# Gated linear attention and two MLPs on one core: alpha of later units in a PSUM bank, the carried state as 112-row blocks, and new shares between the engines

## The chip, the cores and the metric

The kernel runs on 1 core of one Trainium2 chip. The metric is the device time of one execution in microseconds (us), as a median of runs. The kernel before took 1007.21 us, the median of 3 runs between 1004.37 and 1009.0 us.

## What is computed

Inputs are q, k, v and alpha of shape (4 batches, 8 heads, 768 tokens, 48), and four weight matrices. First comes gated linear attention, head by head and token by token, then two MLPs with different activations:

```python
def _attn_ref(q, k, v, alpha) -> np.ndarray:
    B, H, S, D = q.shape
    state = np.zeros((B, H, D, D), dtype=np.float32)
    y = np.zeros_like(q)
    for t in range(S):
        state = alpha[:, :, t, :, None] * state + np.einsum('bhd,bhe->bhde', k[:, :, t], v[:, :, t])
        y[:, :, t] = np.einsum('bhd,bhde->bhe', q[:, :, t], state)
    return y.astype(np.float32)
...
x = np.ascontiguousarray(attn_out.transpose(0, 2, 1, 3)).reshape(B * S, H * D)
h = x @ w_in
g = np.where(h >= 1, h, np.where(h <= -1, 0.0, (h + 1) ** 2 / 4.0))
x = g @ w_out
h = x @ w_in2
out = (h * np.cos(h)) @ w_out2
```

The MLPs have 3072 tokens, a width of 384 and an inner width of 2048. Weights arrive as float64 and are rebuilt on the chip from their two 32-bit halves.

## The kernel before

The 3072 tokens are eight **units** u of 384 tokens, two per batch. Each unit has four **pairs** of heads, so there are 32 pairs, numbered m = 0 to 31; a pair holds its two heads on partitions 0 to 47 and 64 to 111 (the 112 rows of the shapes below), with the tokens along the free axis, as three chunks c of 128 tokens.

A pair runs through these steps (function `attention`). Alpha, k and q are loaded and transposed, so that channels lie on partitions. In the first two units (`TURN`) TensorE (PE) turns them into PSUM banks "h" (L520); in units 2 to 7, pairs 8 to 31, VectorE (DVE) turns them with `turn` (L508) from SBUF to SBUF, alpha to the tile "ta". `forward` (L550) is three scans, running products of alpha per chunk, to the tile F; `ends` takes the last column of each chunk and its reciprocal (fe); `last` (POOL, L576) and `backward` (L582), three reversed scans, make G. Then k is multiplied by G and q by F (`times`, L599, on POOL or DVE), and ScalarE (ACT) squares F and G for an overflow flag (L615). k goes to token order through TensorE (units 0 and 1) or through a DVE transpose and a round trip by DMA (L650, L655, L662). `scores` (L678) multiplies k by q into the banks "sc" (head 0) and "kv" (head 1); a triangular mask turns these into am, on DVE (L688), or by an ACT copy and a POOL product (L691, L694) for the (m, head) in `MASK_POOL`. `outer` (L710) makes k times v per chunk in "kv". The **state** T of a pair is carried from chunk to chunk: ACT scales the kv block of a chunk by its fe (L771 for the first chunk, L779 to the tile kf after that), DVE adds the old state times fe (L782). `within_and_before` makes the output y: per chunk two matmuls of v and am, one per head (L731), and, where there is a state, two of T and q (L736). T is 48 rows by 48 columns at the partitions of its head:

```python
for z in hrows:
    nc.tensor.matmul(
        yb.tile[z, s], lhsT=t.tile[z], rhs=d["tq"][z, s], start=False, stop=True
    )
```

The result y is split into a high part (ACT, L818) and a low part (DVE, L832), both in the reduced format of the matmuls that follow, and 16 rows of another pair are moved in by DMA (L840).

Layer 1 has 16 steps per unit (`step1`), layer 2 the same (`step2`). A step is 9 matmuls for h and 9 for the output (all L871, 128x384), since each product is made of three with high and low parts. Between them a step of layer 1 has an ACT activation (L949) and two DVE instructions (L953, L957), or, for the steps in `ACT_STEPS`, three on ACT and one on DVE (L975); then the split of the result on ACT (L902) and POOL (L907). Layer 1's weights are rebuilt on ACT, DVE and POOL (L345 to L374) while units 0 to 2 run.

The order is made before the kernel is built: class `Order` holds every operation with an engine, an assumed duration, the operations it waits for and the buffers it takes from rings, and places them one by one on the engines. The bank "sc" is a ring of 1, F, G and ta are rings of 1. `SPREAD` adds length behind each pair, which sets how far ahead of the steps that need it a pair is started. The numbers at the top (`SPREAD`, `STEP`, `K_DVE`, `Q_DVE`, `ACT_STEPS`, `MASK_POOL`) and the assumed durations so move instructions, and on the chip each engine takes them strictly in the order that came out. All DMAs are issued by one queue (SP).

Of the kernel before, what the change touches and what calls it, by code (L numbers as in the profile page):

```python
# [30 lines left out]
SPREAD = {None: 29.5, 0: 11.0, 1: 11.0, 2: 14.0, 3: 21.0}  # L31
SLACK = 0.0
STEP = 0.0
# [121 lines left out]
def gla_two_mlps(  # L155
# [51 lines left out]
    NV, NRAW = 4, 4  # L207
# [4 lines left out]
    rings.update({f"T{j}": 4 for j in range(NP)})  # L212
# [38 lines left out]
    v_b = [one.tile([P, CH, 112], F32, name=f"v{i}") for i in range(NV)]  # L251
    raw_b = [one.tile([P, R * D], F32, name=f"raw{i}") for i in range(NRAW)]
# [6 lines left out]
    def prologue():  # L259
# [22 lines left out]
    def weight(layer, kind, f, after=()):  # L282
# [94 lines left out]
        if new:  # L377
            cost = HW2 if kind == "out" else HW3 if layer == 2 else 4 * HW3
            pair_of["op"] = add("sp", cost, fetch, after, new=[rb], lat=LOAD + 1)
# [24 lines left out]
    def early_buffers():  # L404
# [17 lines left out]
        for c in range(CH):  # L422
# [4 lines left out]
            v0_ops.append(add("sp", HW3, load, use=[v0b], lat=LOAD + 1))  # L427

    def attention(m):
# [15 lines left out]
        for x, src in enumerate((alpha, k, q)):  # L445
# [24 lines left out]
            if turned:  # L470
                loads.append([add("sp", HW3, load_tokens, use=[rb], lat=LOAD)])
# [8 lines left out]
        else:  # L480
# [9 lines left out]
            v_ops = [add("sp", 2 * HW3, load_v, new=[vb], lat=LOAD)] * CH  # L490
# [14 lines left out]
        def turn(x, pool_, tag, tb):  # L505
            def fn():
                d[tag] = room(pool_, tag)
                nc.vector.transpose(  # L508
                    out=d[tag].rearrange("p (i r) -> p r i", r=R),
                    in_=d["raw", x].rearrange("p (r d) -> p r d", d=D)[:, :, 0:32],  # L510
                )
# [27 lines left out]
        else:  # L539
            a_src = ab  # L540
            ta, tk = turn(0, p1, "ta", ab), turn(1, p2, "tk", kb)

        def alphas(s):
            return (a_src.tile if turned else d["ta"])[0:K, s]
# [14 lines left out]
        fw = add("dve", CH * (0.35 if turned else 0.48), forward, [ta], new=[fb], use=[a_src])  # L559
# [31 lines left out]
        bw = add("dve", CH * (0.4 if turned else 0.57), backward, [la], use=[a_src, feb, gb])  # L591
# [19 lines left out]
        def square(i, nm):  # L611
            def fn():
                if turned and i == 0:
# [7 lines left out]
        for i, nm, xb in ((0, "F", fb), (1, "G", gb)):  # L621
            fresh = turned and i == 0
# [23 lines left out]
        else:  # L646
# [18 lines left out]
            a = add("sp", QUADS * HW3, write, [a], new=[sb], use=[gb], lat=LOAD + 0.5)  # L665
            ks = add("sp", HW3, read, [a], new=[ksb], use=[sb], lat=LOAD)
# [54 lines left out]

        def within_and_before(cs):

            def fn():
                if cs[0] == 0:
                    yb.tile = ps(tag_y)
                for c in cs:
# [16 lines left out]
                    0.12 + 0.37 * sum(1 if state[c][0] is None else 2 for c in cs),  # L744
# [7 lines left out]
        for c in range(CH):  # L752
# [8 lines left out]
            tb = buf(f"T{j}")  # L761
            r = slice(c * D, (c + 1) * D)
            t = T.get(j)

            def fresh(tb=tb):
                tb.tile = p1.tile([P, D], F32, tag=f"T{j}", name=f"T{j}", bufs=4)
                return tb.tile[0:K]

            if start:
                def first_state(c=c, r=r, fresh=fresh):  # L770
                    nc.scalar.mul(fresh(), kvb.tile[0:K, r], d["fe"][0:K, 0, c:c + 1])  # L771

                T_OP[j] = add("act", 0.185, first_state, [kv], new=[tb], use=[feb, kvb])
            else:
                sb_ = buf("kf")

                def scaled(c=c, r=r, sb_=sb_):
                    sb_.tile = p2.tile([P, D], F32, tag="kf", name="kf")
                    nc.scalar.mul(sb_.tile[0:K], kvb.tile[0:K, r], d["fe"][0:K, 0, c:c + 1])  # L779

# [558 lines left out]
```

## Time and profile before

| what | value |
|---|---|
| time, median of 3 runs | 1007.21 us (1004.37 to 1009.0) |
| the profiled execution: its own time | 1003.58 us |
| the profiled execution: its span | 1001.8 us |
| mean granted TensorE clock | 0.990 of full speed |
| PE, PEld (weight loads) busy | 96%, 89% of the span |
| DVE, ACT, POOL busy | 61%, 55%, 43% |

The profile is of one execution, 3.6 us below the median. Busy shares are means over stages that differ: in the first 57 us only attention runs, then attention and layer 1 run side by side up to about 505 us, then layer 2 and the rest of layer 1. So what an engine means for the time is read from the windows of the rows below, and what a PE instruction costs from the starts in a timeline, since matmuls overlap and a row's mean duration is longer than the distance from one start to the next.

### The profile page before, as it was taken

To read this page: it belongs to the slowest core of one execution; us is meant where nothing else is said; L and a number is where in the kernel's file an instruction comes from. 1 tells how busy PE (TensorE), PEld (TensorE's weight loads), DVE (VectorE), ACT (ScalarE), POOL (GpSimd) and SP (SyncE) were. 2 spreads that over 40 slices of the span, in tenths; PEclk is the share of its full clock that TensorE was granted. 3 is DMA by queue.
4 is the path that set the end of the run, shared out by engine and by line. 5 is a ranking of instruction groups with operands and counts; after the bars stand their busy time and mean duration, and the time that the engine had idled before them with its cause. 6 is when DMAs were issued, how large, how long until landed. Compare 5 with 4: busy or idle time off the path is not lost.

```text
span 1001.8 us, 17336 instructions
## 1 busy us (share of the span) xinstructions
PE 963.5 (96%) x6186; PEld 894.7 (89%) x6186; DVE 613.6 (61%) x1242; ACT 549.1 (55%) x1236; POOL 427.8 (43%) x458
## 2 busy tenths in 40 slices
PE   7897799899999999999999999999999999999997
PEld 5686787789889899889999999899999999999996
DVE  5989999986898568783345777533333333333332
ACT  3557455553344334433335678666666666666664
POOL 3245655654334334342226666534343434242332
PEclk9999799999999999999999999999999999999999
DMA  9765747453555136340031423000000000000000
GB/s 196 154 150 146 159 91 157 110 115 77 131 117 128 36 69 135 81 87 3 9 115 46 128 95 126 25 1 25 1 25 1 25 1 25 1 25 2 24 1 27
DMA packets 113551, 71.81 MB, mean 72 GB/s; under 512 B 71728, under 2 KB 96304, under 8 KB 113456
## 3 DMA queue, kind: packets, MB, share of 16 engines
q1 hardware_dynamic: 113456, 70.62, 29.8%
q8 instruction: 50, 0.82, 0.4%
q14 instruction: 45, 0.37, 0.1%
HBM read 58.79 MB, written 9.44 MB: 68 GB/s over the span
## 4 chain that ended last, share of the span: by engine, by line
PE 74%; DVE 5%; SPq 2%; DMA 2%; ACT 2%; issue 1%; POOL 0%; DVEq 0%; ACTq 0%; POOLq 0%
PE acc L871 30%; PE h L871 25%; PE sc L871 5%; PE kv L871 5%; PE y L871 4%; PE y L731 2%; PE y L736 2%; PE sc L678 1%; SPq L466 1%; DMA w_spare<-in_moe_w_out_dram 1%; PE kv L710 1%; DVE G L582 1%; SPq L655 1%; DVE F L550 0%; DMA raw<-in_q_dram 0%
## 5 line engine op out<-in xcount | busy, mean ns | idle before, releaser
L907 POOL TENSOR_TENSOR gl<-ang,gh 128x384 fp32r<-128x384 f32 x127 | 129.3, 1018 | 234.7 <-ACT gh L902 202.8
L907 POOL TENSOR_TENSOR gl<-r,gh 128x384 fp32r<-128x384 f32 x128 | 132.7, 1037 | 178.4 <-ACT gh L902 146.9
L871 PE MATMUL h<-x,winhi 128*128 128x384 f32 x768 | 199.5, 340 | 4.8 <-DVE r L957 2.8
L871 PEld LDWEIGHTS h<-x,winhi 128*128 128x128 f32 x768 | 138.1, 188 | 10.0 <-DVE r L957 4.2
L871 PE MATMUL acc<-gh,wouthi 128*128 128x384 f32 x384 | 135.3, 352 | 1.7 <-ACT gh L902 0.8
L871 PE MATMUL acc<-gl,wouthi 128*128 128x384 f32 x384 | 130.8, 341 | 2.6 <-POOL gl L907 2.4
L949 ACT ACTIVATE r<-h,half 128x384 f32<-128x384 f32 x119 | 69.0, 580 | 113.9 <-PE h L871 107.3
L871 PE MATMUL h<-x,winlo 128*128 128x384 f32 x384 | 130.0, 339 | 1.3 <-POOL winlo L374 1.3
L871 PE MATMUL acc<-gh,woutlo 128*128 128x384 f32 x384 | 129.9, 338 | 0.0
L902 ACT CAST gh<-r 128x384 fp32r<-128x384 f32 x128 | 65.5, 512 | 97.4 <-DVE r L957 82.7
L953 DVE TENSOR_TENSOR h<-r,h 128x384 f32<-128x384 f32 x119 | 66.5, 559 | 83.7 <-ACT r L949 83.1
L1060 ACT ACTIVATE ang<-ang 128x384 f32<-128x384 f32 x128 | 67.2, 525 | 67.3 <-DVE ang L1055 67.3
L871 PE MATMUL h<-x2s,winhi 128*128 128x384 f32 x402 | 102.3, 335 | 0.6 <-DVE ang L1067 0.5
L871 PE MATMUL acc<-wouthi,gl 128*128 128x384 f32 x288 | 98.1, 341 | 0.3 <-POOL gl L907 0.2
L871 PE MATMUL acc<-wouthi,gh 128*128 128x384 f32 x288 | 97.8, 340 | 0.5 <-ACT gh L902 0.5
L871 PE MATMUL acc<-woutlo,gh 128*128 128x384 f32 x288 | 97.3, 338 | 0.0
L902 ACT CAST gh<-ang 128x384 fp32r<-128x384 f32 x128 | 65.5, 512 | 55.7 <-DVE ang L1067 55.6
L871 PEld LDWEIGHTS acc<-gh,wouthi 128*128 128x128 f32 x384 | 72.6, 189 | 8.2 <-issue 2.1
L871 PEld LDWEIGHTS acc<-gl,wouthi 128*128 128x128 f32 x384 | 72.7, 189 | 4.4 <-POOL gl L907 4.4
L1067 DVE SCALAR_TENSOR_TENSOR ang<-ang,h 128x384 f32<-128x384 f32 x67 | 37.0, 553 | 64.5 <-ACT ang L1063 64.5
L871 PEld LDWEIGHTS h<-x,winlo 128*128 128x128 f32 x384 | 72.0, 188 | 2.3 <-POOL winlo L374 2.3
L871 PEld LDWEIGHTS h<-x2s,winhi 128*128 128x128 f32 x402 | 72.8, 188 | 1.2 <-DVE ang L1067 0.8
(164 smaller groups left out, 2105.4 us busy)
## 6 DMA issues: line engine op xcount, KB each, us to landing
w_raw<-in_moe_w_out_dram SPq DMA_DIRECT2D x18, 384.0 KB, 3.6
scr<-G SPq DMA_DIRECT2D x96, 48.0 KB, 1.9
ks<-scr SPq DMA_DIRECT2D x24, 192.0 KB, 2.7
out_dram<-o SPq DMA_DIRECT2D x24, 192.0 KB, 2.0
v<-in_v_dram SPq DMA_DIRECT2D x56, 72.0 KB, 2.4
w_raw<-in_moe_w_in_dram SPq DMA_DIRECT2D x10, 384.0 KB, 4.0
raw<-in_alpha_dram SPq DMA_DIRECT2D x48, 72.0 KB, 2.1
raw<-in_k_dram SPq DMA_DIRECT2D x48, 72.0 KB, 2.1
```

The costliest lines, as they stand in the source:

```text
L466: nc.sync.dma_start(dst[p0:p0 + 32, 0:n], bass.AP(src.tensor, off, [[R * D, 32], [1, n]]))
L582: nc.vector.tensor_tensor_scan(out=d["G"][0:K, c * C:(c + 1) * C - 1][:, ::-1], data0=alphas(slice(c * C + 1, (c + 1) * C))[:, ::-1], data ...
L655: nc.sync.dma_start(scr[:, 32 * z:32 * z + 32].rearrange("(m i) d -> i m d", i=32), d["G"][32 * z:32 * z + 32].rearrange("p (m d) -> p m d ...
L731: nc.tensor.matmul(yb.tile[z, s], lhsT=vcols(c, z), rhs=am_b[amb.slot][:, e, s], start=True, stop=t is None)
L736: nc.tensor.matmul(yb.tile[z, s], lhsT=t.tile[z], rhs=d["tq"][z, s], start=False, stop=True)
L871: nc.tensor.matmul(o, lhsT=lhs[a], rhs=rhs[b], start=first and i == 0, stop=last and i == 2)
L902: nc.scalar.copy(ghb.tile, g())
L907: eng.tensor_tensor(out=glb.tile, in0=g(), in1=ghb.tile, op=ALU.subtract)
L949: nc.scalar.activation(rb.tile, h.tile[:, 0:N], AF.Relu, bias=half, scale=0.5)
L953: nc.vector.tensor_tensor(out=hh, in0=rb.tile, in1=hh, op=ALU.max)
L1060: nc.scalar.activation(rb.tile, rb.tile, AF.Sin, scale=HALF_TURN)
L1067: nc.vector.scalar_tensor_tensor(out=rb.tile, in0=rb.tile, scalar=1.0, in1=h.tile[:, 0:N], op0=ALU.subtract, op1=ALU.mult)
```

## The change

Four things change.

1. In units 2 to 7 alpha is turned by DVE into the PSUM bank "sc" instead of the SBUF tile "ta", and the six scans of a pair read it there. The bank is the one that the scores of the pair use later, a ring of 1.
2. The state of a pair is one block of 112 rows by 2 x 48 columns, with zeros where rows of one head meet columns of the other. The two state matmuls of a chunk take all 112 rows each; ACT scales head by head, two instructions of 48 rows where there was one of 112, and DVE advances 96 columns where there were 48. The blocks and kf are persistent tiles that POOL sets to zero at the start.
3. The tables are set anew. Pair 6 has k, and pairs 2 and 3 have q, on DVE, and pair 7 has q no longer; step 13 of unit 1 is no longer an ACT step; the masks of POOL go from 7 to 9; for pairs 25, 28, 30 and 31 (`LOW_POOL`) the low part of y is made by an ACT copy and a POOL subtraction; `SPREAD` goes from 29.5 to 25, for unit 2 from 14 to 20, for unit 3 from 21 to 15; assumed durations of DMA issues, scans and y steps are changed. All of these reach the chip as another order alone.
4. The overflow check takes both heads in one pass of 112 rows.

```diff
-SPREAD = {None: 29.5, 0: 11.0, 1: 11.0, 2: 14.0, 3: 21.0}
+SPREAD = {None: 25.0, 0: 11.0, 1: 11.0, 2: 20.0, 3: 15.0}
...
-STEP = 0.0
+STEP = 0.5
...
-K_DVE = (3, 4, 5)
-Q_DVE = (0, 1, 4, 6, 7)
+K_DVE = (3, 4, 5, 6)
+Q_DVE = (0, 1, 2, 3, 4, 6)
...
-ACT_STEPS = ((4, 10, 12, 15), (1, 4, 10, 13, 14))
-MASK_POOL = ((1, 0), (6, 1), (11, 0), (13, 0), (14, 0), (15, 0), (15, 1))
+LOW_POOL = (25, 28, 30, 31)
+ALPHA_BANK = "sc"
+ACT_STEPS = ((4, 10, 12, 15), (1, 4, 10, 14))
+MASK_POOL = ((3, 0), (3, 1), (6, 1), (11, 0), (12, 1), (13, 0), (14, 1), (15, 0), (15, 1))
...
+    t_b = one.tile([P, NP + NTW, 2, D], F32, name="T")
+    kf_b = one.tile([P, 2, 2, D], F32, name="kf")
...
+        nc.gpsimd.memset(t_b, 0.0)
+        nc.gpsimd.memset(kf_b, 0.0)
...
-                d[tag] = room(pool_, tag)
+                if pool_ is None:
+                    tb.tile = ps(tb.tag)
+                    dst = tb.tile[:, 0:N]
+                else:
+                    dst = d[tag] = room(pool_, tag)
                 nc.vector.transpose(
-                    out=d[tag].rearrange("p (i r) -> p r i", r=R),
+                    out=dst.rearrange("p (i r) -> p r i", r=R),
...
-            a_src = ab
-            ta, tk = turn(0, p1, "ta", ab), turn(1, p2, "tk", kb)
+            a_src = buf(ALPHA_BANK)
+            ta, tk = turn(0, None, "alpha", a_src), turn(1, p2, "tk", kb)
...
-                        for z in hrows:
+                        for e, z in enumerate(hrows):
                             nc.tensor.matmul(
-                                yb.tile[z, s], lhsT=t.tile[z], rhs=d["tq"][z, s], start=False, stop=True
+                                yb.tile[z, s], lhsT=state_of(t)[:, e, :], rhs=d["tq"][0:K, s], start=False, stop=True
                             )
...
-                    0.12 + 0.37 * sum(1 if state[c][0] is None else 2 for c in cs),
+                    0.15 + 0.235 * sum(1 if state[c][0] is None else 2 for c in cs),
...
+            def scale_blocks(dst, c=c):
+
+                for e, z in enumerate(hrows):
+                    nc.scalar.mul(dst[z, e, :], kvb.tile[z, c * D:(c + 1) * D], d["fe"][z, 0, c:c + 1])
...
-                    nc.scalar.mul(sb_.tile[0:K], kvb.tile[0:K, r], d["fe"][0:K, 0, c:c + 1])
...
-                        out=fresh(),
-                        in0=t.tile[0:K],
+                        out=state_of(tb),
+                        in0=state_of(t),
                         scalar=d["fe"][0:K, 0, c:c + 1],
-                        in1=sb_.tile[0:K],
+                        in1=kf_b[0:K, sb_.slot],
...
-        lo = add("dve", k_ * dve(N), low, [hi], use=[yb, stb if first else xb])
+        if m in LOW_POOL:
+            ycb = buf("ta")
+            a = add("act", act(N), copied, [hi], new=[ycb], use=[yb])
+            lo = add("pool", k_ * pool(N), low_pool, [a], use=[ycb, stb if first else xb])
+        else:
+            lo = add("dve", k_ * dve(N), low, [hi], use=[yb, stb if first else xb])
```

The order moves at two places that matter below. The first is DVE in the middle of attention, around the scans of one pair of units 2 to 7. A row is a line, an operation, and out<-in; am is the masked scores, ta or sc holds alpha. Before:

```order
L550 SCALAR_TENSOR_TENSOR F<-ta,big 112x128 x3
L563 TENSOR_SCALAR fe<-F 112x3
L953 TENSOR_TENSOR h<-r,h 128x384
L688 TENSOR_TENSOR am_93<-sc,mask 128x384
L688 TENSOR_TENSOR am_93<-kv,mask 128x384
L569 RECIPROCAL fe<-fe 112x3
L957 SCALAR_TENSOR_TENSOR r<-r,h 128x384
L582 SCALAR_TENSOR_TENSOR G<-ta,fe,big 112x127 x3
```

The same place with the change:

```order
L699 TENSOR_TENSOR am_93<-sc,mask 128x384
L519 STREAM_TRANSPOSE sc<-raw_102 128x12x32
L561 SCALAR_TENSOR_TENSOR F<-sc,big 112x128 x3
L574 TENSOR_SCALAR fe<-F 112x3
L970 TENSOR_TENSOR h<-r,h 128x384
L580 RECIPROCAL fe<-fe 112x3
L792 SCALAR_TENSOR_TENSOR T<-T,fe,kf 112x96
L974 SCALAR_TENSOR_TENSOR r<-r,h 128x384
L593 SCALAR_TENSOR_TENSOR G<-sc,fe,big 112x127 x3
```

Before, alpha of a pair stood turned, and its scans had begun, ahead of the masks of the pair in front of it; now the turning of alpha stands behind the mask that empties "sc", and the scans behind that.

The second place is ACT, where the kv blocks of a pair are scaled for two chunks. Before:

```order
L615 ACTIVATE ta,chk<-G 112x384
L615 ACTIVATE ta,chk<-F 112x384
L949 ACTIVATE r<-h,half 128x384
L779 ACTIVATE kf<-kv,fe 112x48 x2
L691 COPY am_94<-sc 128x384
```

With the change:

```order
L626 ACTIVATE ta,chk<-F 112x384
L626 ACTIVATE ta,chk<-G 112x384
L919 CAST gh<-r 128x384
L782 ACTIVATE kf<-kv,fe 48x48 x4
L966 ACTIVATE r<-h,half 128x384
```

Two instructions have become four, in the same place of the queue.

## Rows read from the trace of the kernel before

**Rows 1.** Windows: start:end, length, busy us of PE, PEld, DVE, ACT, POOL; clock, DMA.

```profile
0.00:57.00 57.00, 46.98 (x440) 34.98 (x441) 43.49 (x120) 28.76 (x81) 17.20 (x41) 0.94 0.79 166
...
75.00:225.00 150.00, 132.04 (x877) 112.42 (x876) 141.43 (x270) 82.89 (x201) 87.45 (x88) 0.97 0.59 130
225.00:525.00 300.00, 299.03 (x2080) 269.40 (x2079) 203.42 (x424) 117.80 (x279) 110.44 (x121) 1.00 0.37 82
525.00:1001.80 476.80, 467.41 (x2653) 463.29 (x2651) 209.80 (x397) 310.49 (x655) 203.11 (x202) 1.00 0.10 32
```

**Rows 2.** Waits of PE, 75 to 225 us: who for whom, total us, times, longest.

```profile
PE kv L710 <- DVE am L688: 3.6, 1, 3.6
PE h L871 <- DVE r L957: 2.8, 4, 1.5
...
PE kv L678 <- DVE am L688: 2.1, 1, 2.1
```

**Rows 3.** Timeline of PE, a pair with three states: start us, us, instruction.

```profile
503.34 0.43 PE L731 MATMUL y<-am,v 128*64 128x128 f32 x4
503.70 0.42 PE L736 MATMUL y<-tq,T 48*48 48x128 f32 x4
504.05 0.43 PE L731 MATMUL y<-am,v 128*64 128x128 f32 x4
...
505.48 0.45 PE L871 MATMUL acc<-gh,wouthi 128*128 128x384 f32 x1
```

**Rows 4.** Timeline of PE, a pair with two states.

```profile
422.37 0.65 PE L731 MATMUL y<-am,v 128*64 128x128 f32 x8
422.95 0.42 PE L736 MATMUL y<-tq,T 48*48 48x128 f32 x4
...
424.02 0.62 PE L871 MATMUL h<-x,winhi 128*128 128x384 f32 x2
```

**Rows 5.** Groups by line and form, 75 to 225 us: busy us, mean ns.

```profile
L582 DVE TENSOR_TENSOR_SCAN G<-ta,fe,big 112x127 f32<-112x127 f32 x27 | 20.4, 808 | 2.1 <-DMA scr<-G 2.1
L550 DVE TENSOR_TENSOR_SCAN F<-ta,big 112x128 f32<-112x128 f32 x24 | 14.6, 660 | 0.2 <-POOL tq L599 0.2
L953 DVE TENSOR_TENSOR h<-r,h 128x384 f32<-128x384 f32 x22 | 12.2, 554 | 0.8 <-ACT r L949 0.7
L736 PE MATMUL y<-tq,T 48*48 48x128 f32 x68 | 7.7, 305 | 1.6 <-ACT T L771 1.6
```

**Rows 6.** Groups by line and form, whole span: busy us, mean ns.

```profile
L582 DVE TENSOR_TENSOR_SCAN G<-h,fe,big 112x127 f32<-112x127 f32 x18 | 7.3, 462 | 0.0
L550 DVE TENSOR_TENSOR_SCAN F<-h,big 112x128 f32<-112x128 f32 x18 | 6.3, 405 | 4.2 <-PE h L520 4.2
L953 DVE TENSOR_TENSOR h<-r,h 128x384 f32<-128x384 f32 x119 | 66.5, 559 | 83.7 <-ACT r L949 83.1
L508 DVE STREAM_TRANSPOSE ta<-raw 128x384 f32<-128x384 f32 x24 | 20.7, 862 | 2.5 <-ACT ta L615 2.5
L650 DVE STREAM_TRANSPOSE G<-tk 128x384 f32<-128x384 f32 x24 | 13.5, 563 | 1.9 <-POOL tk L599 1.9
L782 DVE SCALAR_TENSOR_TENSOR T<-T,fe,kf 112x48 f32<-112x48 f32 x64 | 25.0, 391 | 6.0 <-ACT kf L779 4.7
L779 ACT ACTIVATE kf<-kv,fe 112x48 f32<-112x48 f32 x60 | 15.2, 299 | 5.0 <-PE kv L710 5.0
L599 POOL TENSOR_TENSOR tk<-tk,G 112x384 f32<-112x384 f32 x28 | 31.0, 1108 | 19.4 <-DVE G L582 14.7 <-PE h L871 2.8 <-PE acc L871 2.0
```

**Rows 7.** The scans of line 582 by form, whole span: ns min/median/max.

```profile
L582 DVE TENSOR_TENSOR_SCAN G<-ta,fe,big x72: 397/474/3119, 82.5 to 441.0; 112x127 f32<-112x127 f32 x72
L582 DVE TENSOR_TENSOR_SCAN G<-h,fe,big x18: 454/456/481, 6.3 to 55.9; 112x127 f32<-112x127 f32 x18
```

**Rows 8.** Timeline of POOL at the start.

```profile
1.27 0.21 POOL masks.py:65 MEMSET mask<- 128x128 f32 x1
...
6.45 0.19 POOL L576 COPY G<-fe 112x3 f32<-112x3 f32 x1 [3.05 <-DVE fe L569]
```

More of the change, by code (lines that the diff above doesn't have):

```diff
@@ L211, in gla_two_mlps @@
     rings.update({"wy": 2, "wz": 2, "ta": 1, "F": 1, "G": 1, "tq": 2, "stg": 1, "tk": 2, "ks": 2, "am": 2})
-    rings.update({f"T{j}": 4 for j in range(NP)})
+    rings.update({f"T{j}": 1 for j in range(NP)})
+    rings["Tw"] = NTW
     rings.update({"kf": 2, "fe": 3, "r": 3, "gh": 3, "gl": 3, "scr": 3})
@@ L426, in load @@
                 )
-            v0_ops.append(add("sp", HW3, load, use=[v0b], lat=LOAD + 1))
+            v0_ops.append(add("sp", 1.0, load, use=[v0b], lat=LOAD + 1))
     def attention(m):
@@ L470, in attention @@
             if turned:
-                loads.append([add("sp", HW3, load_tokens, use=[rb], lat=LOAD)])
+                loads.append([add("sp", 0.7, load_tokens, use=[rb], lat=LOAD)])
             else:
@@ L488, in load_v @@
                     )
-            v_ops = [add("sp", 2 * HW3, load_v, new=[vb], lat=LOAD)] * CH
+            v_ops = [add("sp", 2 * HW2, load_v, new=[vb], lat=LOAD)] * CH
         def vcols(c, z):
@@ L557, in forward @@
                 )
-        fw = add("dve", CH * (0.35 if turned else 0.48), forward, [ta], new=[fb], use=[a_src])
+        fw = add("dve", CH * 0.35, forward, [ta], new=[fb], use=[a_src])
         def ends():
@@ L589, in backward @@
                 )
-        bw = add("dve", CH * (0.4 if turned else 0.57), backward, [la], use=[a_src, feb, gb])
+        bw = add("dve", CH * 0.4, backward, [la], use=[a_src, feb, gb])
         def times(tag, src, by, direct, pool_, tb, by_buf, after):
@@ L612, in fn @@
             def fn():
-                if turned and i == 0:
+                if i == 0:
                     d["ta"] = room(p1, "ta")
@@ L621, in attention @@
         for i, nm, xb in ((0, "F", fb), (1, "G", gb)):
-            fresh = turned and i == 0
+            fresh = i == 0
             sq.append(
@@ L664, in attention @@
             a = add("dve", dve(N), block, [ksc, sq[1]], use=[gb, kb])
-            a = add("sp", QUADS * HW3, write, [a], new=[sb], use=[gb], lat=LOAD + 0.5)
-            ks = add("sp", HW3, read, [a], new=[ksb], use=[sb], lat=LOAD)
+            a = add("sp", QUADS * HW2, write, [a], new=[sb], use=[gb], lat=LOAD + 0.5)
+            ks = add("sp", 0.9, read, [a], new=[ksb], use=[sb], lat=LOAD)
         hrows = (slice(0, D), slice(64, 64 + D))
@@ L789, in advance @@
                     )
-                a = add("act", 0.185, scaled, [kv], new=[sb_], use=[kvb, feb])
-                T_OP[j] = add("dve", 0.29, advance, [a, T_OP[j]], new=[tb], use=[feb, t, sb_])
+                a = add(
+                    "act", 0.4, lambda sb_=sb_, f=scale_blocks: f(kf_b[:, sb_.slot]), [kv], new=[sb_], use=[kvb, feb]
+                )
+                T_OP[j] = add("dve", 0.34, advance, [a, T_OP[j]], new=[tb], use=[feb, t, sb_])
             T[j] = tb
@@ L820, in copied @@
         def copied():
-            d["yc"] = p1.tile([P, N], F32, tag="ta", name="yc")
-            nc.scalar.copy(d["yc"][0:112], yb.tile[0:112, 0:N])
+            ycb.tile = p1.tile([P, N], F32, tag="ta", name="yc")
+            nc.scalar.copy(ycb.tile[0:112], yb.tile[0:112, 0:N])
         def low_pool():
@@ L1100, in step2 @@
             a = add("dve" if c == 1 else "act", 0.47 if c == 1 else act(N), put, [ops[c]], new=[ob], use=[acc[c]])
-            add("sp", HW2, store, [a], use=[ob], lat=LOAD)
+            add("sp", 0.9, store, [a], use=[ob], lat=LOAD)
     def judge():
```

35 lines of the change are left out of this document (15 added, 20 removed).

## The prediction, written before the changed kernel had run

> **What bounds the kernel now.** The windows come first [rows 1]. PE is busy in nearly all of the span, so nothing that only relieves another engine can pay unless PE waits for it somewhere, and the windows say where it waits. From 225 to 525 us PE is busy 299.0 of 300 us and DVE 203.4: PE alone sets the pace, and a microsecond less on PE is a microsecond less in the time. After 525 us, where no attention is left, PE is busy to within about 9 us of 477, and the change touches nothing there but the place of the overflow check. From 75 to 225 us it is different: PE is busy 132.0 of 150 us, so 18.0 us are waits, while DVE is busy 141.4, 94%. The waits of PE in that stretch name DVE for 8.5 us (the masks for 3.6 and 2.1, a step's product for 2.8) [rows 2], the rest is spread thinly over POOL and ACT. So there DVE sets the pace and PE follows. Before 75 us the attention of units 0 and 1 and the first weights run, DVE is busy 43.5 of the first 57 us, PE 47.0, and PE waits for chains through all engines.
>
> **The state matmuls (PE).** The price of a y step is read from starts, not from durations. In a pair with three states, masks (L731) start at 503.34, states (L736) at 503.70, the next masks at 504.05: each group of four records takes 0.36 us, and the whole step 505.48 - 503.34 = 2.14 us [rows 3]. In a pair with two states the step begins with two mask groups in a row, from 422.37 to 422.95, 0.58 us for both [rows 4]. The second took 0.58 - 0.36 = 0.22 us: without a change of form a group costs 0.22 us, and 0.14 us is what going from 128-row tiles (128*64) to 48-row tiles (48*48), and back, costs each time. With the change the state matmuls take 112 rows and columns of 48, the same form as the masks, so all groups but the last should run at 0.22. A step of six groups then takes 5 x 0.22 + 0.36 = 1.46 us, 0.68 less; one of five takes 4 x 0.22 + 0.36 = 1.24 instead of 1.65 us [rows 4], 0.41 less. Of the 32 pairs half have three states. In 75 to 225 us there are 68 records of L736 [rows 5], 17 states, 7 pairs (three and four): 3 x 0.68 + 4 x 0.41 = 3.7 us. Eight pairs lie before, worth 4.4 us that I count at nothing, since PE waits there anyway; if it does not, they count in full. After 225 us there are 17 pairs (nine and eight): 9 x 0.68 + 8 x 0.41 = **9.4 us**, all on the path.
>
> **The scans (DVE).** From 75 to 225 us the scans of alpha in SBUF keep DVE busy 20.4 us (27 of G, mean 808 ns) and 14.6 us (24 of F, mean 660 ns) [rows 5]. Units 0 and 1 make the same scans from PSUM: 18 of G in 7.3 us and 18 of F in 6.3 us, 0.41 and 0.35 us each [rows 6]. The medians hardly differ, 474 against 456 ns; the difference is a few very long ones, up to 3119 ns from SBUF and none over 481 from PSUM [rows 7]. POOL was less busy when the PSUM ones ran (17.2 of 57 us, against 87.5 of 150), so that alone does not clear them. But L953, which also has one operand in PSUM, runs in the busy stretch at 554 ns, no slower than its 559 over the whole span [rows 5, 6]. So I take the PSUM price: 27 x 0.41 + 24 x 0.35 = 19.4 us, and 35.0 - 19.4 = 15.6 us less on DVE. The 48 more columns of a state cost little: 384 columns take 559 ns, 48 take 391 [rows 6], 0.5 ns a column, so two advances for each of eight pairs cost 16 x 0.024 = 0.4 us. One mask fewer and one step product more on DVE cancel. DVE then needs 141.4 - 15.6 + 0.4 = 126.2 us for this work.
>
> [...]
>
> Turning alpha into PSUM has no row. Below it is a transpose with a plain output, 563 ns, above it the present one, 862 ns [rows 6], raised once more by the ratio of these two, to 1.32 us. I keep 862, since input and output pattern stay the same. The upper end costs the nine pairs (27 scans of G) 9 x 0.46 = 4.1 us in the stretch.
>
> **What 75 to 225 us becomes.** PE needs 132.0 - 3.7 = 128.3 us, DVE 126.2. If all of PE's waits went, the stretch would take 128.3, a gain of 21.7; if none went, 146.3, a gain of 3.7. DVE now loses 150 - 141.4 = 8.6 us to its own waits; I let it lose the same again, since loads and ACT's queue stay: 126.2 + 8.6 = 134.8 us, a gain of **15.2 us**. The new order also puts the first y of unit 2 behind 228 matmuls of steps instead of 165 and with it some of DVE's work into the stretch where DVE is busy 203 of 300 us; I add nothing for that.
>
> **What I cost at nothing.** 80 more ACT instructions of about 0.3 us [rows 6] lie where ACT is busy 82.9 of 150 and 117.8 of 300 us [rows 1]; uncovered they put 0.6 us per pair between L710 and the states, with DVE's advance and PE's y behind them. The four low parts on POOL go from 0.55 us on DVE to an ACT copy and about 1.1 us on POOL, a microsecond longer for four pairs. Zeroing 960 columns on POOL, between 0.6 and 1.6 us by the 0.21 us for 128, fits in the 3.05 us that POOL waits before its first use [rows 8]. The shares of k, q and masks in units 0 and 1 move about 0.6 us to DVE net, which is not full there. No DMA is added. The overflow check loses two short DVE instructions.
>
> **The sum.** 15.2 + 9.4 = 24.6 us off the profiled execution's own 1003.58 us is 979.0. That execution was 3.6 us below the median shown, so I forecast a median of **982.6 us**.
>
> **The rivals.**
> - *DVE was not the brake.* The stretch is held by loads and by queues in fixed order, and a lighter DVE waits longer instead. For it: PE waited for DVE by name for 8.5 of the 18.0 us only [rows 2]. Then 3.7 + 9.4 = 13.1 us, 990.5, as a median 994.
> - *Everything goes.* All 18.0 us of waits vanish and the early pairs count: 21.7 + 9.4 + 4.4 = 35.5 us, 968.1, as a median 971.7. For it: after the change neither engine is full. Against it: they share fixed orders, with chains between them.
> - *The bank ties the pairs together (slower).* Alpha can now be turned only when the mask has emptied "sc", and the next scores need that bank back. The chain from scores to scores is a mask of 384 columns as L953, 0.56, turning 0.86, F 1.05, G 1.22, k on POOL 1.11, and between them two short DVE instructions, up to 0.39 as L782, and a POOL copy of 0.19 [rows 6, 8]: 5.8 us, with the scores and nine hand-offs some 7.5 as my estimate. The order leaves no more than 33 to 45 matmuls between scores in seven places; at 467.4 us for 2653 [rows 1] these are 5.8 to 7.9 us, and a little attention. Each DVE piece also queues behind step products of 0.55 us, and behind the waiting transpose stand the scans and the products of steps that PE needs. Such a place can lose 3 us, seven of them 21 us, which brings the time to about 1000. From 1.3 us a pair, over 24 pairs, the gain is gone; at 2 us it is 1003.6 - 24.6 + 48 = 1027. Against it: in PE's stretch most pairs lie 60 to 130 matmuls apart.
> - *The 112-row blocks do not run side by side (slower).* Then a state group takes 0.36 us twice, 80 groups cost 28 us more, of which 21 after 75 us, and the 13.1 us of PE do not come: 1003.6 - 11.5 + 21 = 1013, as a median 1017. Against it: the masks already run so, with 128 rows, at the pace of the 48-row states [rows 3]. [...]
>
> **How the numbers follow.** I give the forecast 0.62, DVE not the brake 0.17, everything 0.10, the tied bank 0.08 (over half of it only eating the gain), and the blocks 0.03. A difference below 0.5%, 5 us, cannot be told from no change. The first three are all faster: 0.89. The tied bank near break-even gives same 0.05; its worse half and the blocks give slower 0.06. The range reaches from 968, everything gone in a run like the profiled one, to 999, past the second case and the dear transpose.
>
> **What would show it.** In the profile after, L751 (the states) should start 0.22 us after the masks of its chunk, and a whole y step take 1.46 or 1.24 us. Scans from "sc" should have a mean near 460 and 405 ns with none over 600. PE's idle time from 75 to about 210 us should be about 6 us and not 18. I am wrong on the states if the distance is 0.36, on the scans if long ones remain, on the bank if PE waits before L689 or DVE before L519 by microseconds in many places after 225 us, and on the brake if DVE idles more while PE's waits stay.

## The result, and the profile after

The changed kernel takes **979.66 us** (median of 4 runs, 974.75 to 980.37) against 1007.85 us for the kernel before on the same chip: a ratio of 0.972, 95% interval 0.970 to 0.975. The forecast was 982.6 us, the range 968 to 999. The profiled execution took 979.92 us, its span 978.1, against a forecast of 979.0.

The windows of the changed kernel, in the columns of [rows 1]:

```profile
0.00:57.00 57.00, 41.62 (x381) 33.90 (x382) 38.55 (x108) 29.57 (x84) 15.32 (x38) 0.94 0.75 154
...
75.00:225.00 150.00, 142.01 (x970) 130.00 (x969) 130.03 (x262) 92.00 (x218) 85.08 (x88) 1.00 0.56 122
225.00:525.00 300.00, 298.64 (x2165) 280.98 (x2165) 207.69 (x456) 146.17 (x355) 127.38 (x141) 1.00 0.40 91
525.00:978.10 453.10, 446.15 (x2543) 444.63 (x2541) 201.02 (x380) 301.55 (x633) 190.63 (x190) 1.00 0.10 32
```

From 75 to 225 us PE idles 8.0 us and not 18.0, DVE is busy 130.0 and not 141.4 us, so DVE's own idle time there grew from 8.6 to 20.0 us. In the first 57 us PE is busy 5.4 us less than before.

The waits of PE in 75 to 225 us answer to [rows 2]:

```profile
PE h L888 <- DVE r L974: 3.1, 3, 1.4
PE h L888 <- DVE r L992: 1.8, 3, 0.9
PE h L888 <- ACT winhi L377: 1.2, 1, 1.2
```

The waits for masks (3.6 and 2.1 us) are gone; what is left for DVE is products of steps, 4.9 us.

The y steps, on PE's timeline: one of two states, then one of three, against [rows 4] and [rows 3]. L746 are the masks, L751 the states.

```profile
298.53 0.65 PE L746 MATMUL y<-am,v 128*64 128x128 f32 x8
299.01 0.39 PE L751 MATMUL y<-tq,T 112*48 112x128 f32 x4
...
299.77 0.37 PE L689 MATMUL sc<-tq,tk 48*128 48x128 f32 x1
...
313.00 0.43 PE L746 MATMUL y<-am,v 128*64 128x128 f32 x4
313.27 0.39 PE L751 MATMUL y<-tq,T 112*48 112x128 f32 x4
313.49 0.39 PE L746 MATMUL y<-am,v 128*48 128x128 f32 x4
...
314.47 0.37 PE L689 MATMUL sc<-tq,tk 48*128 48x128 f32 x1
```

The steps take 299.77 - 298.53 = 1.24 us and 314.47 - 313.00 = 1.47 us, where they took 1.65 and 2.14. Inside, a group of four starts 0.22 us after the last.

The scans by form over the whole span, against [rows 7] (ns min/median/max):

```profile
L593 DVE TENSOR_TENSOR_SCAN G<-sc,fe,big x72: 450/457/482, 87.6 to 470.8; 112x127 f32<-112x127 f32 x72
L561 DVE TENSOR_TENSOR_SCAN F<-sc,big x72: 358/397/426, 82.0 to 465.1; 112x128 f32<-112x128 f32 x72
```

No scan from the bank takes over 482 ns; from SBUF they went up to 3119. The DVE groups of 75 to 225 us, against [rows 5], with the rebuilding of weights beside them:

```profile
L356 DVE TENSOR_SCALAR wz<-wy 128x384 int32<-128x384 int32 x23 | 16.0, 715 | 0.2
L360 DVE SCALAR_TENSOR_TENSOR wz<-wy,wz 128x384 int32<-128x384 int32 x24 | 14.3, 619 | 0.0
L366 DVE SCALAR_TENSOR_TENSOR wz<-w_spare,wz 128x384 uint32<-128x384 uint32 x13 | 10.9, 859 | 0.0
L593 DVE TENSOR_TENSOR_SCAN G<-sc,fe,big 112x127 f32<-112x127 f32 x21 | 8.5, 460 | 0.0
...
L561 DVE TENSOR_TENSOR_SCAN F<-sc,big 112x128 f32<-112x128 f32 x21 | 7.3, 402 | 0.0
L519 DVE STREAM_TRANSPOSE tk<-raw 128x384 f32<-128x384 f32 x7 | 6.2, 882 | 0.3 <-DMA raw<-in_k_dram 0.3
...
L519 DVE STREAM_TRANSPOSE sc<-raw 128x384 f32<-128x384 f32 x7 | 4.1, 585 | 0.0
```

The same weight lines in the kernel before, same stretch:

```profile
L353 DVE SCALAR_TENSOR_TENSOR wz<-wy,wz 128x384 int32<-128x384 int32 x23 | 14.3, 653 | 0.0
...
L349 DVE TENSOR_SCALAR wz<-wy 128x384 int32<-128x384 int32 x23 | 11.4, 513 | 0.0
...
L359 DVE SCALAR_TENSOR_TENSOR wz<-w_spare,wz 128x384 uint32<-128x384 uint32 x12 | 7.3, 618 | 0.0
```

Two things stand out. Turning alpha into the bank takes 585 ns, where turning k into SBUF in the same order takes 882. And two of the weight instructions, which the change does not touch, became longer: 715 ns instead of 513, 859 instead of 618. The one between them did not: 619 ns, where it took 653.

**Where the time came from.** To compare two executions, take the start of the nth matmul of 128x384 (L871, now L888), that is, how far the MLP steps have come (us from the span's start, from the two traces):

| step matmul | 1st | 151st | 201st | 551st | 701st | 1901st | 2601st | 4601st |
|---|---|---|---|---|---|---|---|---|
| before | 57.7 | 98.1 | 118.3 | 210.0 | 242.8 | 514.7 | 641.9 | 993.3 |
| after | 66.9 | 102.8 | 111.9 | 193.8 | 228.2 | 495.4 | 618.2 | 969.7 |
| difference | +9.2 | +4.7 | -6.4 | -16.2 | -14.6 | -19.3 | -23.7 | -23.6 |

The first step comes 9.2 us later. Between the 151st and the 201st matmul 11.1 us come back at once, until the 551st another 9.8; 4.7 come by the 1901st (the end of attention) and 4.4 at the passage to layer 2, where before the rebuilding of weights and the overflow check met PE. Behind it nothing changes.

The table counts steps alone, and the two orders put different amounts of attention in front of a step. In front of the 1st step matmul PE has made the y of 7 pairs, where it had made 6; in front of the 701st of 14 and not 15, and the scores of 15 pairs and not 17. So a part of the 14.6 us at the 701st is work put off. Run 1 below, with the y steps as long as in the kernel before and the order of the changed one, takes 276.3 us from the 701st to the 1901st, where the kernel before takes 271.9: about 4.4 us were put off, and some 10 us are the stretch's own gain. The two profiled executions are 23.7 us apart, the medians 28.2, since the profiled execution of the kernel before was 3.6 us below the median that stood with it.

### The profile page after: what moved, and what is told of

Its sections match the earlier page's. It is cut to its first block, busy times and chain, and to the rows that moved or that the text cites. A ratio compares the mean times of both kernels' runs of the same rounds, so it can differ in the third digit from the quotient of the medians.

```text
span 978.1 us, 17438 instructions
## 1 busy us (share of the span) xinstructions
PE 943.6 (96%) x6186; PEld 902.2 (92%) x6186; DVE 592.0 (61%) x1237; ACT 580.9 (59%) x1318; POOL 427.1 (44%) x464
## 4 chain that ended last, share of the span: by engine, by line
PE 84%; DVE 6%; DMA 3%; ACT 2%; issue 2%; SPq 2%; POOL 0%; DVEq 0%; POOLq 0%; ACTq 0%
PE acc L888 33%; PE h L888 27%; PE sc L888 5%; PE kv L888 5%; PE y L888 5%; PE y L746 2%; PE sc L689 2%; PE h L531 2%; PE y L751 1%; PE kv L721 1%; DVE wz L356 1%; DMA raw<-in_alpha_dram 1%; DMA w_raw<-in_moe_w_in_dram 1%; SPq L473 1%; DMA ks<-scr 1%
## 5 line engine op out<-in xcount | busy, mean ns | idle before, releaser
L888 PE MATMUL h<-x,winhi 128*128 128x384 f32 x768 | 198.6, 339 | 6.2 <-DVE r L974 3.1
L888 PEld LDWEIGHTS h<-x,winhi 128*128 128x128 f32 x768 | 137.8, 188 | 10.4 <-DVE r L974 3.9
L888 PE MATMUL acc<-gh,wouthi 128*128 128x384 f32 x384 | 135.8, 354 | 0.0
L888 PE MATMUL acc<-gl,wouthi 128*128 128x384 f32 x384 | 130.0, 338 | 0.3 <-POOL gl L924 0.3
L888 PE MATMUL acc<-gh,woutlo 128*128 128x384 f32 x384 | 130.0, 339 | 0.0
L888 PE MATMUL h<-x,winlo 128*128 128x384 f32 x384 | 129.0, 336 | 0.6 <-POOL winlo L381 0.5
L888 PE MATMUL h<-x2s,winhi 128*128 128x384 f32 x402 | 103.0, 337 | 0.0
L888 PE MATMUL acc<-wouthi,gl 128*128 128x384 f32 x288 | 97.4, 338 | 0.3 <-POOL gl L924 0.3
L888 PE MATMUL acc<-wouthi,gh 128*128 128x384 f32 x288 | 96.9, 337 | 0.0
L888 PE MATMUL acc<-woutlo,gh 128*128 128x384 f32 x288 | 96.9, 336 | 0.0
L888 PEld LDWEIGHTS acc<-gh,wouthi 128*128 128x128 f32 x384 | 71.9, 187 | 6.5 <-issue 2.8
L888 PEld LDWEIGHTS h<-x2s,winhi 128*128 128x128 f32 x402 | 73.4, 188 | 0.0
L888 PEld LDWEIGHTS h<-x,winlo 128*128 128x128 f32 x384 | 72.1, 188 | 1.2 <-POOL winlo L381 1.2
L888 PEld LDWEIGHTS acc<-gl,wouthi 128*128 128x128 f32 x384 | 72.1, 188 | 0.8 <-POOL gl L924 0.8
```

The lines of the kernel that those rows point to most:

```text
L888: nc.tensor.matmul(o, lhsT=lhs[a], rhs=rhs[b], start=first and i == 0, stop=last and i == 2)
```

## The experiments

All medians are beside runs of the kernel before on the same chip; "over the changed kernel" is the difference of the two ratios to the kernel before (0.9722 for the changed one) times 1006.6 us. Each ratio is certain to 2 to 3 us, a difference of two to some 3.5.

**1. The form of the state matmuls.**

```
-  yb.tile[z, s], lhsT=state_of(t)[:, e, :], rhs=d["tq"][0:K, s], ...
+  yb.tile[z, s], lhsT=state_of(t)[z, e, :], rhs=d["tq"][z, s], ...
```

> The changed kernel, with only the state matmuls of y back to 48 rows and columns (48*48 in place of 112*48); state blocks, tables and the order of every instruction stay. Theory (each change of form between masks and states costs PE 0.14 us): the y steps take 2.14 us (three states) and 1.65 us (two) again instead of the 1.46 and 1.24 that the changed kernel shows; 17 pairs after 225 us cost 9.4 us more, the pairs before up to 8 us, part of it hidden: 9 to 17 us over the changed kernel, 989 to 997 us. Rival (the form is worth nothing in the end, because PE waits elsewhere): y steps at 2.14 and 1.65 us, time within 3 us of the changed kernel's 979.7.

992.07 us, ratio 0.9855 [0.9826, 0.9884]: 13.4 us over the changed kernel. Steps of y take 1.65 and 2.15 us again. By the starts of step matmuls, this kernel is behind the changed one by 4.6 us at the 1st, 4.3 at the 151st, 4.3 at the 551st, 5.7 at the 701st and 14.8 at the 1901st. So in this order the form is worth almost nothing from 75 to 225 us, and 9.1 us behind the 701st matmul, at 228 us. How much of the 4.6 us before the first step it is worth is not shown: the granted clock of this execution is lower there (0.81 from 57 to 75 us, where the changed kernel had 0.92, and 0.91 against 0.94 before that), and the execution is 2.7 us above the median of its kernel.

**2. Alpha in SBUF, with the planner told so.** The source of the scans becomes "ta", and the planner's ring and assumed scan durations with it; the planner then makes another order.

```
-  a_src = buf(ALPHA_BANK)
-  ta, tk = turn(0, None, "alpha", a_src), turn(1, p2, "tk", kb)
+  a_src = ab
+  ta, tk = turn(0, p1, "ta", ab), turn(1, p2, "tk", kb)
```

> The changed kernel with alpha of units 2 to 7 turned into SBUF and scanned there again; the wide states and the new tables stay. Theory (the long scans are a matter of having both operands in SBUF, and DVE paces PE in the stretch of about 75 to 225 us): scans of 600 to 3000 ns are back on the turned units, their means at 0.6 to 0.8 us, the transposes of alpha at 0.86 instead of 0.58 us, DVE needs 15 us more for the same work in that stretch, and the kernel comes 8 to 16 us above the changed kernel: 988 to 996 us. Rival (DVE was not the brake): the long scans are back, but the time stays within 3 us of 979.7.

1010.07 us, ratio 1.0029 [1.0011, 1.0047]: 31 us over the changed kernel, far more than either theory. PE's waits from 95 to 180 us:

```profile
PE acc L888 <- DVE x L1020: 8.1, 1, 8.1
PE sc L689 <- POOL tk L610: 7.2, 1, 7.2
PE h L888 <- DVE r L974: 3.4, 3, 2.5
PE kv L721 <- DVE am L699: 3.0, 2, 2.2
```

Two stalls of 7.2 and 8.1 us stand one behind the other, and the 50 step matmuls from the 151st to the 201st take 31.0 us instead of 9.1. The order changed with the place, so this run does not price the operand's place. Run 5 does.

**3 and 4. Is DVE the brake?** The transpose of q of units 2 to 7 is issued twice, in the kernel before and in the changed one.

```
+  if x == 2:
+      nc.vector.transpose(out=d[tag]..., in_=d["raw", x]...)
```

> The kernel before with the transpose of q of units 2 to 7 issued twice in a row on VectorE (the second writes the same values), nothing else moved: 0.86 us more of DVE for each of 24 pairs, about nine of them in 75 to 225 us. Theory (DVE paces that stretch): 6 to 9 us slower than the kernel before, almost all of it gathered by matmul 900 and none of it after. Rival (DVE is not the brake, the stretch is held by loads and fixed queues): less than 2 us.

> The same doubled transpose of q in the changed kernel: 0.86 us more of DVE for each of 24 pairs. Theory (with the scans short, DVE has slack and paces much less of the stretch): 0 to 4 us slower than the changed kernel, clearly less than the same edit costs the kernel before. Rival (DVE still paces the stretch as before): 6 to 9 us slower here too.

The kernel before becomes 1014.16 us, ratio 1.0080 [1.0054, 1.0105], 8.1 us slower; the changed one 980.15 us, ratio 0.9741 [0.9712, 0.9769], 1.9 us more, within the uncertainty of no change. So some 21 us more on DVE (24 transposes of 0.87) cost 8.1 us before and next to nothing now: DVE was a brake, and is almost none any more. One part of the first expectation missed: of the 10.8 us in the profiled executions 4.8 had come by the 701st matmul and another 5.9 between it and the 1901st. PE is busy 294.0 of the 300 us after 225 us there, instead of 299.0, and waits for DVE's masks for 3.7 us behind the 701st matmul: there, too, DVE held PE up in places.

**5. The place of alpha alone.** The order of every engine is that of the changed kernel, only the tile differs; the squares go to a bf16 tile so that "ta" is free.

```
-  tb.tile = ps(tb.tag)
-  dst = tb.tile[:, 0:N]
+  dst = d["ta"] = room(p1, "ta")
```

> The changed kernel with alpha of units 2 to 7 turned into the SBUF tile ta in place of the bank sc and scanned from there, every instruction of every engine in the same order as in the changed kernel (the squares of the overflow check are written to a bf16 tile of their own). So, unlike the kernel that gave the planner alpha in SBUF, only the place of the operand differs. Theory (long scans cost DVE time that PE waits for, in the stretch of about 75 to 225 us): the transposes of alpha take 0.86 us again and scans of over 600 ns are back, 7 pairs in that stretch cost DVE some 10 to 14 us, of which the idle time DVE has there hides a part: 4 to 14 us over the changed kernel, 984 to 994 us. Rival (the place is worth nothing in itself, the 30 us of the other kernel came from its order): within 3 us of 979.7.

982.61 us, ratio 0.9778 [0.9754, 0.9803]: 5.6 us over the changed kernel, near the low end of the theory. Its DVE groups of 75 to 225 us:

```profile
L593 DVE TENSOR_TENSOR_SCAN G<-ta,fe,big 112x127 f32<-112x127 f32 x21 | 13.7, 705 | 0.0
...
L357 DVE TENSOR_SCALAR wz<-wy 128x384 int32<-128x384 int32 x23 | 13.3, 597 | 0.0
L561 DVE TENSOR_TENSOR_SCAN F<-ta,big 112x128 f32<-112x128 f32 x21 | 12.0, 625 | 0.0
...
L519 DVE STREAM_TRANSPOSE ta<-raw 128x384 f32<-128x384 f32 x7 | 6.1, 865 | 0.0
```

The scans cost 25.7 us and not 15.8, the transposes 6.1 and not 4.1: 11.9 us more. The first weight instruction costs 13.3 us and not 16.0. Its window:

```profile
75.00:225.00 150.00, 140.82 (x947) 128.94 (x944) 135.02 (x258) 91.30 (x216) 87.53 (x87) 0.99 0.53 118
```

DVE is busy 135.0 us against 130.0, but the window holds a slightly different set of instructions. Since the order is the same, instructions can be compared one by one instead. Of the 409 that DVE starts before the 701st step matmul of the changed kernel, the scans and the transposes of alpha take 12.6 us more here, all the others together 3.9 us less. The 701st matmul comes only 2.4 us later (another 2.9 are lost by the 1901st): most of what DVE does more falls into time in which it was idle in the changed kernel. Over the whole kernel DVE does 25 us more, and the time grows by 5.6.

**6 to 8. Old tables in the changed kernel.** All of them (SPREAD, STEP, K_DVE, Q_DVE, LOW_POOL, ACT_STEPS, MASK_POOL), then K_DVE, Q_DVE and MASK_POOL, then K_DVE and Q_DVE alone.

```
-K_DVE = (3, 4, 5, 6)
-Q_DVE = (0, 1, 2, 3, 4, 6)
+K_DVE = (3, 4, 5)
+Q_DVE = (0, 1, 4, 6, 7)
```

> The changed kernel with the tables as before (shares of k, q and masks, SPREAD, STEP, the steps' shares, no low parts on POOL); the wide states and alpha in the bank stay. Theory (the two parts of the change pay by themselves, the tables only move the attention a little): 975 to 990 us; the first step matmul again near 58 to 60 us instead of 66.9 and the weights of the second layer meeting attention again, about 4 us lost there. Rival (the tables carry much of the gain, since alpha in the bank ties scores to scores and the old order leaves these too close): 990 to 1010 us, with PE waiting before the scores or DVE before the transpose of alpha.

> The changed kernel with the shares of k, q and masks of units 0 and 1 between DVE, POOL and ACT as before (K_DVE, Q_DVE, MASK_POOL), the rest of the change kept; steps then begin after five pairs have finished y's instead of seven. Theory (these shares and the order that follows from them delay the first steps by 9 us, and the stretch behind does not need that): the first step matmul at 57 to 62 us, 2 to 8 us faster than the changed kernel. Rival (the attention left over comes later and costs the same, or meets the DVE-bound stretch): within 3 us, or slower.

> The changed kernel with only the shares of k and q as before (K_DVE, Q_DVE), the masks' shares as in the change. Theory (the delay of the start comes from the shares of k and q): first step matmul at 57 to 62 us, 2 to 8 us faster than the changed kernel. Rival (it comes from the masks on POOL, or from the wide states): start at 65 to 68 us and the time within 3 us.

999.64 us (ratio 0.9947 [0.9929, 0.9965]), 1007.34 us (1.0016 [0.9999, 1.0034]) and 999.93 us (0.9943 [0.9923, 0.9962]): 23, 30 and 22 us over the changed kernel. In all three my theory fell. The rival held in the first two; in the third neither did, since the first step came at 69.6 us, later than in the changed kernel. (In the second the steps begin behind the y of six pairs by the trace, not five.) With all tables old, the first step comes 2.4 us earlier than in the changed kernel, not 7; by the 151st matmul this kernel is 3.4 us ahead, by the 201st 28.2 behind. The waits of the second one (old shares of k, q and masks) from 95 to 180 us, and its windows:

```profile
PE sc L689 <- POOL tq L610: 11.6, 1, 11.6
PE kv L721 <- DVE wz L366: 11.6, 1, 11.6
PE sc L689 <- POOL tk L610: 8.0, 2, 5.2
```

```profile
105.00:120.00 15.00, 1.72 (x12) 1.43 (x12) 13.58 (x30) 5.63 (x15) 6.87 (x8) 0.62 0.78 160
120.00:135.00 15.00, 4.61 (x44) 3.64 (x44) 11.89 (x29) 6.41 (x18) 6.03 (x7) 0.61 0.76 167
135.00:150.00 15.00, 7.67 (x41) 7.22 (x42) 11.17 (x26) 6.33 (x19) 8.85 (x9) 0.52 0.73 177
```

PE is busy 14.0 of these 45 us, and the granted clock is down to 0.52 to 0.62. This led to a new theory: the jam comes where the order leaves PE too few step matmuls between the scores of the first pairs of unit 2.

**9 to 11. The spacing of the scores.** One table put back at a time: MASK_POOL; STEP (to 0.0); SPREAD.

> The changed kernel with only the masks' shares as before (MASK_POOL). In its PE order 54, 75 and 120 step matmuls lie between the 9th, 10th, 11th and 12th scores (114, 84 and 111 in the changed kernel; 36 and 36 for the first and third in the kernel with the old shares of k and q, which jams). Theory (the jam of 100 to 140 us comes where fewer than about 40 step matmuls lie between the scores of the first pairs of unit 2; otherwise the order is free): no PE idle time of over 3.5 us in one place, within 5 us of the changed kernel, and up to 4 us faster since the first steps come earlier. Rival (any change of this order jams, the tables are a lottery): 10 to 30 us slower.

> The changed kernel with STEP back to 0.0 alone. In its PE order 36, 162 and 45 step matmuls lie between the 9th, 10th, 11th and 12th scores. Theory (fewer than about 40 step matmuls between the first scores of unit 2 jam): PE idle for 5 us and more in one piece between 105 and 135 us, the clock halved behind it, 10 to 25 us slower than the changed kernel. Rival (STEP is a small term of the planner's, the spacing of scores is not the cause): within 4 us.

> The changed kernel with SPREAD as before alone. In its PE order 141, 93, 96 and 36 step matmuls lie between the 9th to 13th scores. Theory (spacing of the first scores decides): no jam between 100 and 150 us; units 2 and 3 are spread otherwise, at most a short wait at the 36 behind the 12th scores; within 6 us of the changed kernel. Rival (a lottery): 10 to 30 us slower.

987.01 us (ratio 0.9799 [0.9771, 0.9826]), 998.46 us (0.9916 [0.9891, 0.9940]) and 988.58 us (0.9816 [0.9788, 0.9844]): 7.8, 19.5 and 9.5 us over the changed kernel. Only the STEP run jams early, as expected. Its two stalls of over 6 us are both of the outer products (L721), the first with 6.1 us put down to the DMA of ks, not scores waiting. The columns are the step matmuls that the order puts between the scores of pairs 8, 9, 10 and 11, and the time from the 151st to the 201st step matmul in the trace:

| kernel | 8 to 9 | 9 to 10 | 10 to 11 | 151st to 201st, us |
|---|---|---|---|---|
| changed kernel, runs 1 and 5 | 114 | 84 | 111 | 9.1, 9.2, 9.2 |
| old masks | 54 | 75 | 120 | 9.9 |
| old SPREAD | 141 | 93 | 96 | 12.3 |
| STEP 0 | 36 | 162 | 45 | 25.7 |
| old k, q | 36 | 162 | 36 | 28.1 |
| alpha in SBUF, planned so | 36 | 162 | 36 | 31.0 |
| all tables old | 36 | 225 | 33 | 40.7 |
| old k, q, masks | 27 | 0 | 0 | 53.3 |
| before | 201 | 9 | 84 | 20.2 |

With 54 or more there is no jam in this piece, with 36 or fewer always. The kernel before has its own stall there, 3.6 us for a mask of pair 8 [rows 2], and a granted clock of 0.50 behind it (105 to 114 us; 0.70 in the mean from 105 to 120 us). No run moves the spacing alone, so this is a pattern over these kernels and not a shown cause. And it does not explain all: the kernels with old masks and old SPREAD lose 7.8 and 9.5 us, more than the 5 and 6 I had allowed, and lose them further on, the first with 6.0 us in one wait for DVE at 153 us, which I had said would not come. The kernels with old SPREAD and with STEP 0 also lose the 4.4 us at the passage to layer 2 again: from the 1901st to the 2601st matmul they take 127.2 and 127.3 us, as the kernel before (127.2), and the changed kernel 122.8. So putting back either of these two tables, which move no work between engines, is enough to lose them.

**12. The wide states alone, in the order of before.** Everything else is the kernel before, the order of every engine included, but for the overflow check in one pass.

```
-  fresh(), in0=t.tile[0:K], in1=sb_.tile[0:K]
+  out=state_of(tb), in0=state_of(t), in1=kf_b[0:K, sb_.slot]
```

> The kernel before, its tables, costs and order of every engine kept, with the states as blocks of 112 rows alone (blocks with zeros, two ACT scalings per state, state matmuls 112*48); alpha stays in SBUF. Theory (a step of y costs 1.46 or 1.24 us instead of 2.14 or 1.65 wherever PE is never short of work; where PE waits for others the gain is lost in waits): 9 to 10 us from the 17 pairs behind about matmul 600, up to 4 us from the first pairs and nothing from those between: 9 to 14 us faster than the kernel before, about 992 to 997 us. Rival (it is worth more here, since the early stretch gains too): 15 to 18 us. Rival (two scalings per state on ACT delay the states): less than 8 us.

1008.46 us, ratio 1.0020 [1.0001, 1.0038]: no gain at all, as the second rival had it. Steps of y do take 1.24 and 1.46 us after 225 us. The waits of PE from 57 to 225 us show one price:

```profile
PE kv L721 <- DVE am L699: 3.6, 1, 3.6
PE y L751 <- ACT T L782: 2.9, 1, 2.9
...
PE kv L689 <- ACT kf L782: 1.7, 1, 1.7
```

PE waits for the states themselves, which ACT now scales in two instructions where the order was made for one. By the 551st step matmul this kernel is 9.5 us behind the kernel before; up to the 1901st it wins back 4.3, and PE is busy 295.9 of 300 us after 225 us, where it was 299.0. The clock shows another price: 0.91 from 75 to 225 us, where it was 0.97. How the 9.5 us divide between the waits and the clock is not shown.

## Why the prediction was right, and where it was not

**The state matmuls** came out as worked. The group without a change of form costs 0.22 us, a y step 1.24 and 1.47 us, and run 1 prices the pairs behind 228 us at 9.1 us, where 9.4 were forecast. Run 1, with the change of form put back, has steps of 1.65 and 2.15 us, which agrees with the 0.14 us per change; why a change costs this is not shown. The two smaller terms were off: the 3.7 us of 75 to 225 us are 1.4 in run 1, and the first pairs, counted at nothing, may count, up to the 4.6 us of run 1, of which the lower clock (0.81 against 0.92 from 57 to 75 us) may have taken a part; no run separates it.

**The scans** were right in their durations (0.46 and 0.40 us, none over 482 ns) and too dear in what they save: 5.6 us in run 5, 2.4 of them by the 701st matmul, where the forecast put 11.5 us into 75 to 225 us. The step that failed is "I let it lose the same again": DVE was to set the pace still, with 8.6 us of idle time. It idles 20.0 us, PE is busy 142.0 of the 150 us, and a doubled transpose costs nearly nothing (run 4). The lighter DVE stopped being the brake, so the last part of its saving bought no time.

A smaller part went to other instructions, since the long instructions are not a property of a scan. In the kernel before, between 57 and 525 us, of the 72 scans of G from SBUF the 34 without a POOL instruction beside them took at most 482 ns; the 38 with one took 940 ns in the mean, up to 3119. In the changed kernel 53 scans of G have POOL beside them and take 461 ns in the mean. The first weight instruction lengthened already before (L349: 345 ns in the mean without POOL beside, 561 with it) and does so more now (L356: 9 without POOL took 347 ns in the mean, 18 with POOL 862, up to 2141). The longest in the kernel before stands in this row of DVE instructions, with POOL's of the same time behind them:

```profile
110.59 1.02 DVE L353 SCALAR_TENSOR_TENSOR wz<-wy,wz 128x384 int32<-128x384 int32 x2
111.53 1.01 DVE L359 SCALAR_TENSOR_TENSOR wz<-w_raw,wz 128x384 uint32<-128x384 uint32 x2
112.46 4.61 DVE L582 TENSOR_TENSOR_SCAN G<-ta,fe,big 112x127 f32<-112x127 f32 x3
...
110.00 2.59 POOL L576 COPY G<-fe 112x3 f32<-112x3 f32 x1
112.55 1.19 POOL L599 TENSOR_TENSOR tq<-tq,F 112x384 f32<-112x384 f32 x1
113.70 1.02 POOL L907 TENSOR_TENSOR gl<-r,gh 128x384 fp32r<-128x384 f32 x1
114.68 1.02 POOL L374 TENSOR_TENSOR winlo<-wz,winhi 128x384 fp32r<-128x384 f32 x1
```

and in the changed kernel:

```profile
110.21 3.19 DVE L366 SCALAR_TENSOR_TENSOR wz<-w_spare,wz 128x384 uint32<-128x384 uint32 x1
...
110.02 1.99 POOL L924 TENSOR_TENSOR gl<-r,gh 128x384 fp32r<-128x384 f32 x2
111.97 1.01 POOL L381 TENSOR_TENSOR winlo<-wz,winhi 128x384 fp32r<-128x384 f32 x1
```

In both, three POOL instructions follow each other without a pause, and the long DVE instruction (in the first case the second of the three scans, 112.86 to 115.97 us) ends soon after the third has ended. It goes the other way too: the POOL copy of three columns ahead of them, 0.19 us in the median of its 32, takes 2.59 us while DVE runs weight instructions back to back.

The rows have a pattern: the instructions with an operand in PSUM take as long beside POOL as without it. Beside POOL or not, the scans with alpha in PSUM stay below 483 ns, and in the kernel before the masks below 574 and the products L953 below 618 (between 57 and 525 us 557 ns in the mean without POOL beside, 559 with it). Those that lengthen have all their operands in SBUF, but not all that have them there lengthen so: the transposes of alpha into SBUF in the kernel before took 842 ns in the mean without POOL beside and 866 with it. What sets them apart is not shown. I had seen POOL's share [rows 1] and set it aside, because L953 did not suffer; but that line has one operand in PSUM. With the scans out of SBUF, others took longer: in run 5, where alpha is in SBUF again, the scans and the transposes of alpha take 12.6 us more and all the others 3.9 us less.

An operand in PSUM costs the scans nothing that shows: the medians of G are 457 ns from PSUM, 470 from SBUF in run 5.

**Turning alpha** into the bank was held at 862 ns and takes 585, near the lower bound.

**DVE as the brake** holds for the kernel before alone: 8.1 us for a doubled transpose there, 1.9 after. "Everything goes" did not happen, 8 of 18 us of waits are left. "The bank ties the pairs together" did not happen in this kernel. The same kind of jam does in its neighbours, but also with alpha in SBUF (run 2), so it does not need the bank; whether the bank makes it worse is not shown. My price for it, 7.5 us from scores to scores, is too small at the start of unit 2: in the old-shares run the scores of pairs 8, 9 and 10 start at 96.1, 109.2 and 128.5 us with 27 and 0 matmuls between them.

**What was costed at nothing** is the step that failed as an argument. "The shares of k, q and masks in units 0 and 1 move about 0.6 us to DVE" is true as work, and putting the shares of k and q back costs 22 us; STEP, which moves no work at all, costs 19.5 and all tables 23. A table that moves next to no work moves the order, and in these kernels the order decided whether PE jams between 100 and 140 us.

So the number came near partly by luck. In the profiled executions some 10 us come by the 701st matmul, once the work put off is taken out, where 15.2 were forecast; 9.1 come from the form behind it, where 9.4 were forecast; and 4.4 come at the passage to layer 2, where nothing was. The 5 us that the first stretch lacks and the 4.4 that nobody had counted nearly cancel. The first stretch is itself a sum of things not forecast: the first step comes 9.2 us later (what from is open: 64.5 us with all tables old, 59.2 with the wide states alone), and between the 151st and the 201st matmul the kernel before takes 11.1 us longer, with its stall, a granted clock of 0.50 behind it and the y of one more pair.

The parts do not add up to one another: form 13.4 and place 5.6 us leave 9 of the 28 to the order, yet the form alone in the old order gives nothing, and both parts with the old tables give 5. Each is worth what the order lets it be. Not separated are the assumed durations of DMAs, LOW_POOL and ACT_STEPS. What alpha in the bank is worth in the order of before stays open: the bank is in use then, so no run has it.

## What to carry to other kernels

Price a saving at the engine it relieves, then ask at what point that engine stops being the brake: here DVE, 94% busy, was relieved and its idle time went from 8.6 to 20.0 us of 150. Ask also who else lengthens beside the same engine's work: here scans of G from SBUF took 940 ns in the mean beside POOL and at most 482 without it, and taking the scans out passed a part on to others (3.9 of 12.6 us in run 5). Where an order is written by a planner, a table that moves no work can cost more than the work of the change; read from the order how much filling stands between the links of the longest chain, before trusting a sum of durations. Count the work put off, too, before reading a lead in steps as a gain. And test a part in the fixed order of the kernel it belongs to (run 5), since letting the planner react (run 2) measured the planner.

## What the runs showed of the hardware

A DVE transpose of 128x384 with a strided output takes 585 ns into PSUM and, for k in the same kernel and stretch, 882 ns into SBUF with the same pattern; alpha itself takes 865 ns into SBUF in run 5. With a plain output into SBUF a transpose took 563 [rows 6]. So neither the pattern alone nor SBUF alone was dear here, but the two together. And a stall of PE can cost more than its length: in the kernel before, behind the stall of 3.6 us, the granted clock was 0.50 from 105 to 114 us and the step matmuls from 111.0 to 113.6 us start 0.32 us apart, where those from 114.3 to 119.3 us, at a clock of 1.00, start 0.17 us apart. The old-shares run had a granted clock of 0.52 to 0.62 for the 45 us in which PE was busy 14.0.
